# Attention in 128-token blocks ahead of an MLP: loads, transposes and scores by block, with rings of tiles

## The chip, the cores and the metric

One core of one Trainium2 chip. The metric is the device time of one execution in microseconds (us), the median of several fast runs. The span of a profile is shorter than the measured time of the same execution: 378.2 against 379.9 us before.

## The reference

Sliding-window attention with a linear distance bias (8 batches, 8 heads, 576 tokens, head size 64, window 128), whose output goes into an MLP with a squared ReLU (4608 tokens, 512 to 2048 to 512).

```python
scores = scale * np.matmul(q, k.transpose(0, 1, 3, 2))
mask = (rel >= 0) & (rel < 128)                      # rel = query - key position
scores = np.where(mask, scores + bias[None], -1e9)   # bias = -slope[h] * |rel|
attn = softmax(scores)
x = np.matmul(attn, v)            # -> (4608, 512), heads side by side
h = np.maximum(x @ w_in, 0.0)
out = (h * h) @ w_out
```

## The kernel before

The program is a list of small tasks (one instruction each, with the engine, an estimated length in ns, dependencies and a priority key, lower first). A list scheduler in the kernel file puts them in an order once, at build time; every engine then runs its instructions in exactly that order, and waits in place when the data is not there. So the estimated lengths decide the order, and only the order. PE is the matrix engine; it writes its results to PSUM, which this program uses as eight banks. An "eviction" is the copy of a finished bank by VectorE or ScalarE.

K and Q of a batch come in as two halves of four heads, 72 partitions of 8 tokens each. VectorE reorders them, PE transposes them in 16-fold pieces of 72 columns, and VectorE and ScalarE copy each finished bank out.

```python
def load(key, ns, emit, deps=(), acq=()):
    return plan.add({"POOL": 1000.0}, key, emit, deps, acq, dma=ns)   # figures for the scheduler
# K/Q half: 1900 ns; V, 128 tokens: 2050 ns; a quarter of w_in 3100 ns, of w_out 3300 ns
...
base_t = s_b - 256 - 16 if b > 1 else s_b - 4000 + 1000 * b      # key of a batch's transposes
base_s = s_b - 128 - 16 if b else -2000                          # key of its scores
...
for r in range(R):                         # R = 8 transposes of 72 columns fill one bank
    nc.tensor.transpose(slot.tile[:, r * RP:(r + 1) * RP],
                        sl.tile[:, r, 2 * cj:2 * cj + 2].rearrange("p h d -> p (h d)"), ident[0:RP, 0:RP])
...
add_evac(kT[p2][c][:, 0:S], [last, t_pad[p2]], 0, 128, t_k[c], {"DVE": dve(576)})   # after the last of the eight
...
nc.tensor.matmul(slot.tile[:, 0:2 * nq].rearrange("p (c q) -> p c q", c=2),         # scores, by key block
                 kT[p2][c][:, kb * 128:(kb + 1) * 128], qp[p2][c][:, :, kb * 128:kb * 128 + nq], ...)
```

The MLP works on groups of 512 tokens: matmuls `h` (w_in), ReLU on ScalarE, square on VectorE, matmuls `o` (w_out). Group 0 needs the tokens of blocks 0 to 3 of batch 0. The attention of later batches is woven between the matmuls of earlier MLP groups. The eight banks are shared out as two each for `h`, `o`, scores (`s`) and everything else of attention (`att`).

The softmax here doesn't subtract the row's maximum and nothing guards it: scores larger than these inputs give would overflow.

## Time and profile before

| | before |
|---|---|
| measured, first three runs | 379.1 us (377.2 to 379.2) |
| span of the profile | 378.2 us |
| first MLP matmul starts | 53.0 us |
| PE streaming work in all (see below) | 318.7 us |
| of it before the first MLP matmul | 12.5 us |
| PE time lost after the first MLP matmul | 15.1 us |
| of that, ahead of input transposes | 3.8 us |

"PE streaming work" and "time lost" are worked out from the start times of the matmuls in the trace. From 60 to 280 us the usual distance from one start to the next is 216 ns for 512 columns, 56 for 128 and 29 for 65, which is N/2.4 + 2.5 ns within a nanosecond or so. The 72-column transposes of the kernel before are the exception: mostly 35 ns apart where the formula has 32.5, so that some 1.3 us of its streaming counts as lost here. The sum by the formula over all matmuls is the streaming work; what the distance to the next start has more than that is lost. This tells more than the busy share, because in the trace, which models the ends of matmuls, one counts as busy for some 0.17 us beyond its streaming (0.38 us for 512 columns, 0.22 for 128).

These lines are from the page of the kernel before: busy time by engine; PE in 40 slices of the span (a 9 is 90% or more); the engines' shares of the chain that ended last.

```profile
PE 343.4 (91%) x2560; PEld 178.6 (47%) x2560; DVE 231.6 (61%) x620; ACT 199.7 (53%) x381; POOL 75.1 (20%) x103
...
PE   0567589989999999999999999999999999999995
...
PE 79%; DVE 10%; ACT 6%; DMA 2%; issue 2%; POOL 0%; ACTq 0%; POOLq 0%
```

PE is busy in nearly the whole span except the first six slices, which are 57 us. The same by stretches (length, then the busy us of PE, weight loads, VectorE, ScalarE and GpSimd with counts, the clock, DMA):

```profile
core 0: us, PE busy (x) PEld busy (x) DVE busy (x) ACT busy (x) POOL busy (x), PEclk, DMA share, GB/s
0.00:53.00 53.00, 27.62 (x242) 16.59 (x243) 37.80 (x93) 23.09 (x45) 36.75 (x56) 0.82 1.52 167
...
60.00:300.00 240.00, 235.01 (x1876) 123.83 (x1874) 168.51 (x454) 143.30 (x275) 36.83 (x45) 1.00 0.45 63
```

From 60 to 300 us PE is busy for 235.0 of 240 us. The first 53 us hold 242 of 2560 matmuls. What they wait for is in the timeline of VectorE (start, length, instruction). `xT` is the output of attention for one block of tokens; the reordering copies `r_` belong to batch 1's transposition:

```profile
35.62 0.41 DVE L466 COPY xT<-xp 128x512 bf16<-128x512 bf16 x1
35.95 0.68 DVE L327 COPY r_445<-q_70 72x2048 bf16<-72x2048 bf16 x1
36.55 0.87 DVE L327 COPY r_462<-k_71 72x2048 bf16<-72x2048 bf16 x1
...
52.47 0.42 DVE L466 COPY xT<-xp 128x512 bf16<-128x512 bf16 x1 [0.33 <-PE xp L459]
```

The copy at 35.6 us is the third of the four blocks that group 0 needs. The fourth is copied out only at 52.5 us: between them the engines reorder, transpose and copy out batch 1. The first MLP matmul follows at once (timeline of PE):

```profile
52.98 0.61 PE L493 MATMUL h<-xT,w_in_sb 128*128 128x512 bf16 x1
```

These are the first rows of the list of PE's waits from 60 to 300 us (who waited for whom: us in total, times, longest). It shows small, scattered waits:

```profile
engine line waited for: us in total, times, longest us
PE pv L424 <- DVE qp_3_77 L357: 0.9, 1, 0.9
PE pv L424 <- DVE xT L466: 0.5, 1, 0.5
...
```

### The profile page before, as it was taken

How to read it: one execution, taken by the hardware profiler on the slowest of the kernel's cores; microseconds unless marked ns; L12 is line 12 of the kernel's file. 1: busy time of each engine (PE TensorE's matmuls, PEld its weight loads, DVE VectorE, ACT ScalarE, POOL GpSimd, SP SyncE). 2: the span in 40 equal slices, each digit the busy share in tenths (PEclk: the TensorE clock that was granted, in tenths of full speed). 3: DMA queues.
4: the chain of work that ended last, by engine and by line, in shares of the span. 5: the costliest groups of instructions: out<-in, count | busy, mean ns of one | idle time of the engine just before them, and what ended most of it. 6: DMA issues, size and time to landing. Idle time of an engine off the chain costs nothing.

```text
span 378.2 us, 6568 instructions
## 1 busy us (share of the span) xinstructions
PE 343.4 (91%) x2560; PEld 178.6 (47%) x2560; DVE 231.6 (61%) x620; ACT 199.7 (53%) x381; POOL 75.1 (20%) x103
## 2 busy tenths in 40 slices
PE   0567589989999999999999999999999999999995
PEld 0324345545455545555555554555555554444442
DVE  5878568767687777657775677476767754222200
ACT  1373447545574757347654656475657743434411
POOL 8995422203112112120211020101000000000000
PEclk9998569999999999999999999999999999999999
DMA  7999995839364717562919260531310001100112
GB/s 100 147 204 161 205 172 24 111 45 162 79 62 64 97 11 105 88 88 42 112 22 126 43 79 4 83 44 30 20 57 10 21 29 45 38 29 28 55 57 83
DMA packets 59742, 28.22 MB, mean 75 GB/s; under 512 B 41792, under 2 KB 55104, under 8 KB 59712
## 3 DMA queue, kind: packets, MB, share of 16 engines
q0 software_dynamic: 54528, 18.37, 49.2%
q1 hardware_dynamic: 5184, 9.44, 6.8%
q8 instruction: 20, 0.33, 0.4%
q14 instruction: 10, 0.08, 0.1%
HBM read 36.70 MB, written 9.44 MB: 122 GB/s over the span
## 4 chain that ended last, share of the span: by engine, by line
PE 79%; DVE 10%; ACT 6%; DMA 2%; issue 2%; POOL 0%; ACTq 0%; POOLq 0%
PE o L522 31%; PE h L493 29%; PE ps_s L384 7%; PE pv L424 5%; PE tp L343 4%; DMA k_71<-in_k_dram 2%; PE xp L459 2%; ACT P_91 L395 1%; DVE qp_1_75 L357 1%; DVE qp_2_76 L357 1%; DVE qp_0_74 L357 1%; ACT qp_2_76 L359 1%; ACT rt L501 1%; DVE qp_1_79 L357 1%; DVE qp_0_78 L357 1%
## 5 line engine op out<-in xcount | busy, mean ns | idle before, releaser
L493 PE MATMUL h<-xT,w_in_sb 128*128 128x512 bf16 x576 | 188.4, 380 | 0.1
L522 PE MATMUL o<-w_out_sb,g 128*128 128x512 bf16 x576 | 183.6, 379 | 0.5 <-ACT osb L533 0.3
L501 ACT ACTIVATE rt<-h 128x512 bf16<-128x512 f32 x144 | 85.5, 599 | 75.1 <-PE h L493 64.1
L507 DVE TENSOR_TENSOR g<-rt 128x512 bf16<-128x512 bf16 x144 | 59.3, 416 | 49.9 <-ACT rt L501 48.1
L522 PEld LDWEIGHTS <-g 128*128 128x128 bf16 x576 | 54.3, 98 | 40.4 <-issue 2.5
L493 PEld LDWEIGHTS <-w_in_sb 128*128 128x128 bf16 x576 | 53.0, 98 | 31.6 <-issue 2.1
L533 ACT ACTIVATE osb<-o 128x512 f32<-128x512 f32 x36 | 21.4, 597 | 33.3 <-PE o L522 27.8
L440 DVE RECIPROCAL rec<-pv 128x4 f32<-128x4 f32 (+1 forms) x80 | 13.2, 175 | 32.4 <-PE pv L424 18.9
L290 POOL DMA_DIRECT2D vt_73<-in_v_dram x20 | 17.4, 876 | 52.8 <-PE pv L424 31.5
L279 POOL DMA_DIRECT2D q_70<-in_q_dram x16 | 12.7, 795 | 72.1 <-DVE r_2514 L327 9.9
L395 ACT ACTIVATE P_91<-ps_s 128x512 bf16<-128x512 f32 (+2 forms) x40 | 20.0, 515 | 10.5 <-PE ps_s L384 10.2
L290 POOL DMA_DIRECT2D vt_72<-in_v_dram x20 | 17.6, 883 | 35.6 <-PE pv L424 27.2
L395 ACT ACTIVATE P_93<-ps_s 128x512 bf16<-128x512 f32 (+2 forms) x40 | 19.5, 516 | 9.2 <-PE ps_s L384 8.9
L395 ACT ACTIVATE P_92<-ps_s 128x512 bf16<-128x512 f32 (+2 forms) x40 | 19.5, 515 | 7.1 <-PE ps_s L384 6.3
L395 ACT ACTIVATE P_90<-ps_s 128x512 bf16<-128x512 f32 (+2 forms) x40 | 19.4, 516 | 5.5 <-PE ps_s L384 5.0
L466 DVE COPY xT<-xp 128x512 bf16<-128x512 bf16 (+1 forms) x40 | 15.7, 394 | 8.5 <-PE xp L459 6.2
L424 PEld LDWEIGHTS <-P_93 128*128 128x128 bf16 x144 | 13.7, 101 | 12.7 <-issue 3.5
L424 PEld LDWEIGHTS <-P_90 128*128 128x128 bf16 x144 | 13.9, 102 | 11.4 <-issue 2.9
L424 PEld LDWEIGHTS <-P_91 128*128 128x128 bf16 x144 | 13.6, 100 | 11.4 <-issue 2.2
L424 PEld LDWEIGHTS <-P_92 128*128 128x128 bf16 x144 | 13.4, 99 | 10.2 <-issue 1.0
L459 PE MATMUL xp<-ident,x_94 128*128 128x128 bf16 x80 | 17.2, 227 | 0.7 <-DVE x_94 L445 0.6
L407 DVE TENSOR_TENSOR P_91<-P_91,masks 128x512 bf16<-128x512 bf16 (+2 forms) x40 | 14.0, 363 | 5.7 <-ACT P_91 L395 5.3
(200 smaller groups left out, 555.3 us busy)
## 6 DMA issues: line engine op xcount, KB each, us to landing
out_dram<-osb SPq DMA_DIRECT2D x36, 256.0 KB, 2.0
k_71<-in_k_dram POOLq DMA_DIRECT2D x16, 288.0 KB, 6.7
q_70<-in_q_dram POOLq DMA_DIRECT2D x16, 288.0 KB, 5.5
vt_72<-in_v_dram POOLq DMA_DIRECT2D x16, 128.0 KB, 6.0
w_in_sb<-in_moe_w_in_dram POOLq DMA_DIRECT2D x4, 512.0 KB, 8.2
vt_73<-in_v_dram POOLq DMA_DIRECT2D x16, 128.0 KB, 5.3
w_out_sb<-in_moe_w_out_dram POOLq DMA_DIRECT2D x4, 512.0 KB, 11.0
vt_72<-in_v_dram POOLq DMA_DIRECT2D x4, 64.0 KB, 4.7
```

Source lines behind the costliest of these rows:

```text
L290: nc.gpsimd.dma_start(vt[i][0:n, kb, :, 0:D], v[b, :, kb * 128:kb * 128 + n, :].rearrange("h s d -> s h d"))
L357: nc.vector.tensor_copy(o, s_)
L384: nc.tensor.matmul(slot.tile[:, 0:2 * nq].rearrange("p (c q) -> p c q", c=2), kT[p2][c][:, kb * 128:(kb + 1) * 128], qp[p2][c][:, :, kb * ...
L395: nc.scalar.activation(Pt[sP.idx][:, 2 * c:2 * c + 2, 0:nq], slot.tile[:, 0:2 * nq].rearrange("p (c q) -> p c q", c=2), AF.Exp, bias=0.0, ...
L424: nc.tensor.matmul(slot.tile[:, hi * (D + 1):(hi + 1) * (D + 1)], Pt[sp.idx][:, h, off:off + 128], vt[i][:, kk, h, :], start=st, stop=en)
L459: nc.tensor.transpose(slot.tile[:, c * 128:(c + 1) * 128], xt[sx.idx][:, c * 128:(c + 1) * 128], ident)
L466: nc.vector.tensor_copy(xT[:, :, t0:t0 + n], slot.tile[:, 0:512].rearrange("p (c t) -> p c t", c=C)[:, :, 0:n])
L493: nc.tensor.matmul(slot.tile, w_in_sb[:, cc, fc * 128:(fc + 1) * 128], xT[:, cc, g * 512:(g + 1) * 512], start=cc == 0, stop=cc == C - 1)
L501: nc.scalar.activation(srt.tile, slot.tile, AF.Relu, bias=0.0, scale=1.0)
L507: nc.vector.tensor_tensor(sg.tile[:, fc, :], srt.tile, srt.tile, op=ALU.mult)
L522: nc.tensor.matmul(slot.tile, sg.tile[:, fc, t * 128:(t + 1) * 128], w_out_sb[:, fc, :], start=fc == 0, stop=fc == FCB - 1)
L533: nc.scalar.activation(so.tile, slot.tile, AF.Copy)
```

## The change

The intent: stream attention in blocks of 128 tokens, so that the first output tokens, and with them the MLP, start early. K, Q and V of a block come in natural order (128 tokens on 128 partitions). Eight transposes of 128 columns, K's four and Q's four, fill one bank. Scores go by query block, so that a block needs only its own K and the K before it. All tiles are small rings. The core of the diff, with cuts marked by `...` and comments added:

```diff
-    q8 = const.tile([RP, H, R * D], BF16)
-    k8 = const.tile([RP, H, R * D], BF16)
...
+    size = {"kn": 4, "qn": 4, "v": 6, "kT": 4, "qp": 3, "P": 3, "x": 2}
+    kn = ring("kn", size["kn"], [128, d_model])
...
-        return plan.add({"POOL": 1000.0}, key, emit, deps, acq, dma=ns)
+        return plan.add({"POOL": 900.0}, key, emit, deps, acq, dma=ns)
-            t_win[n] = load(key + n, 3100.0, emit)
+            t_win[n] = load(key + n, 2550.0, emit)
...
+                nc.gpsimd.dma_start(o, src[b, :, kb * 128:kb * 128 + n, :].rearrange("h s d -> s h d"))
+            t_in[m, nm] = load(key + 0.01 * i, 1050.0 * n / 128, emit, ...)
...
+        due = (b * S + kb * 128 + n) / 4 - 192 - 150
...
+        for i in range(2 * C):                       # K's four, then Q's four, one bank
+                nc.tensor.transpose(slot.tile[:, i * 128:(i + 1) * 128], src[:, (i % C) * 128:(i % C + 1) * 128], ident)
+            if i == C - 1:
+                last_k = last
+        t_k = plan.add(both if first else {"DVE": both["DVE"]}, due - 56, evac_k, [last_k], [], [slot])
...
-                        kT[p2][c][:, kb * 128:(kb + 1) * 128],
-                        qp[p2][c][:, :, kb * 128:kb * 128 + nq],
+            for part, mk in parts:                   # the key block before, and this one
+                        kT[sk_of[mk].idx][:, c, :], qp[sq.idx][:, c, :, 0:n], start=True, stop=True)
...
+        slot_x = Slot("o" if first else "att")       # batch 0 borrows the MLP's banks
```

It also gives the scheduler new figures for loads: 1050 ns for 128 tokens where V had 2050, 2550 for a weight quarter where it had 3100 and 3300, 900 for an issue where it had 1000. The diff changes other figures too (a matmul N/2.4 + 1.5 ns where it had + 3, the constants 800 and 1300 where they had 2500 and 3000), lets either VectorE or ScalarE make batch 0's evictions, and drops some clearing of tiles on GpSimd.

## The prediction

> **What bounds the kernel now.** The page shows PE busy 91% of 378 us; from 60 to 300 us the stretch table has it busy 235.0 of 240 us at full clock. In the timeline warm matmuls start about 216 ns (512 columns), 56 ns (128), 32 ns (72) and 30 ns (65) apart, as the Trainium skill states ("TensorE: Matmul & The Clock Gate", Back-to-back issue gap: N/2.4 + 2.5 ns). Summed with that spacing (estimate): MLP 1152 x 216 = 248 us, scores 27.7, weighted values 17.0, input transposes 16.6, output transposes 8.9: about 318 us. So some 60 us of the span is not streaming.
>
> Where it lies: the first MLP matmul starts at 53.0 us. Before it PE has done only about 12.7 us of warm work (128 transposes, 28 scores, 69 values, 16 output transposes): 40 us lost. After it about 16 us are lost in gaps and cold clock, and 3.7 us are the tail. There the chain of waits runs over K loads, the 72x2048 reorder copies (0.68 us each, one 3.08 us) and the 576-column strided evictions (0.75 us DVE, 0.65 us ACT): batch 0 needs all heads of all 576 tokens before its first score, and the whole transposition of batch 1 (34 to 50 us) goes in front of the first MLP matmul.
>
> **The change.** Removes 32 reorder copies (24 us of DVE), 512 transposes of 72 columns, 64 DVE and 32 ACT evictions (48 and 21 us). Adds 320 transposes of 128 columns (17.8 us of PE against 16.6) and 120 evictions of up to 512 columns (0.42 us DVE, 0.6 us ACT, like the xT and exp instructions now). Scores become 288 matmuls of half the width for 160: same columns. DVE falls by some 35 us; PE's sum becomes about 320 us: nothing won there. K and Q now move as 128-byte packets like V: 110,592 instead of 36,864. In the trace they take 40 ns, but with several loads queued one engine starts one each 15 to 16 ns: about 1 us a load, like the 0.88-0.96 us in which POOL issues one. 120 loads need some 110 us of 300: no new bottleneck, but a block costs 2.9 us of issue at the start.
>
> **The critical part: the start.** Block 0 needs only its K and Q (landed near 7 us), transposes, evictions and masks: first exp near 8.5 us (21.4 now), first output tokens near 14. Then a block needs 4 exps of 0.6 us and an eviction on ACT (3 us), and about 4 us of shared DVE work, against 2.9 us of loads: 3.5 to 4 us a block. Four blocks feed group 0: first MLP matmul near 28 us, w_in's first quarter landed before that. PE has then done 9 us. Left are 311 us of streaming, the tail of 3.7 and about 14 us lost: cold clock, ACT and DVE shared by batch 1's attention and the first MLP groups and smaller gaps. 28 + 311 + 18 = 357 us: 22 us (6%) faster. Range 349 to 366. Chances: faster 0.94, same 0.05, slower 0.01.
>
> **What would show it.** First MLP matmul at 25 to 32 us; no 72-partition copies; DVE busy near 195 us; PE busy over 95% from 60 to 300 us; streaming sum within 2 us of before; SWDGE packets about 115,000 or more; POOL about 120 us.
>
> **What would make it wrong.** 128-byte loads slower at the start (30 ns apart instead of 15), which pushes w_in past 28 us; POOL issuing slower while DVE works; PE in program order stalling on a late block or on DVE and ACT between 28 and 60 us; w_out, issued behind batch 1's 15 loads, landing after 45 us.

## The result, and the profile after

365.8 us (four runs, 365.7 to 366.0), against 378.4 us before: the ratio is 0.967, with a 95% interval of 0.964 to 0.970. A ratio here is the mean time of one kernel's fast runs over the mean of the other's in the same rounds, so it is not quite the ratio of the medians quoted. The change is 12.6 us faster; 22 us had been forecast, and the time lies 0.2 us inside the upper end of the range.

| | predicted | before | after |
|---|---|---|---|
| time | 357 (349 to 366) | 378.4 us | 365.8 us |
| first MLP matmul | 25 to 32 us | 53.0 us | 29.5 us |
| streaming work in all | within 2 us of before | 318.7 us | 320.6 us |
| of it before the first MLP matmul | 9 us | 12.5 us | 8.7 us |
| lost after the first MLP matmul | about 14 us | 15.1 us | 19.0 us |
| of that, ahead of input transposes | not told | 3.8 us | 13.8 us in 39 places |
| VectorE busy | near 195 us | 231.6 us | 193.8 us |
| GpSimd busy | about 120 us | 75.1 us | 108.4 us |

The "39" counts places where more than 0.15 us were lost. Of these, 35 stand ahead of one of Q's transposes, in 34 of the 35 blocks whose transposes follow the first MLP matmul; what is lost ahead of Q's transposes is 12.1 us. The other four are K's of block 5 (1.6 us, of which 1.0 for the load of its K). The page of the changed kernel:

```profile
PE 338.9 (93%) x2496; PEld 187.5 (51%) x2496; DVE 193.8 (53%) x593; ACT 205.1 (56%) x394; POOL 108.4 (30%) x137
...
PE   2677899999999999999999999999999999999995
...
PE 76%; issue 7%; POOL 5%; DMA 4%; DVE 4%; ACT 2%; POOLq 0%; ACTq 0%
```

PE shows 7 to 8 tenths from the third slice on and reaches a 9 with the sixth, that is from 45.5 us, where the kernel before does so from 57. The DMA queue that GpSimd feeds carries 116,736 packets where it had 54,528, at the same bytes. By stretches, with the columns of before:

```profile
0.00:29.50 29.50, 16.00 (x160) 11.54 (x160) 17.40 (x61) 18.31 (x39) 23.60 (x35) 0.97 1.48 138
...
60.00:300.00 240.00, 234.76 (x1826) 132.82 (x1825) 143.46 (x439) 146.56 (x282) 65.86 (x80) 1.00 0.70 68
```

The first stretch is 23.5 us shorter. But from 60 to 300 us PE is busy for 234.8 us, hardly other than the 235.0 of before, although VectorE has 25 us less to do there. The start, in the timelines of VectorE, ScalarE and PE:

```profile
16.25 0.41 DVE L280 COPY xT<-xp 128x512 bf16<-128x512 bf16 x1
...
24.23 0.60 ACT L282 ACTIVATE xT<-xp 128x512 bf16<-128x512 bf16 x1
26.94 0.60 ACT L282 ACTIVATE xT<-xp 128x512 bf16<-128x512 bf16 x1
28.83 0.60 ACT L282 ACTIVATE xT<-xp 128x512 bf16<-128x512 bf16 x1 [1.29 <-PE pv L378]
...
29.48 0.58 PE L450 MATMUL h<-xT,w_in_sb 128*128 128x512 bf16 x1 [0.47 <-ACT xT L282]
```

The fourth block's output comes at 28.8 us instead of 52.5. And this is the whole list of PE's waits from 60 to 300 us, with the same columns as before:

```profile
PE tp L301 <- DVE kT_86 L280: 1.1, 4, 0.3
PE tp L301 <- DVE kT_85 L280: 1.0, 4, 0.3
PE tp L301 <- DVE kT_84 L280: 0.7, 3, 0.3
PE tp L301 <- DVE kT_87 L280: 0.5, 2, 0.3
```

Scattered waits have given way to a single kind: an input transpose waits for VectorE's copy of `kT`. One such place, in the timeline without the weight loads (cuts marked by `...`; `tp<-ident,kn_72` is the last of K's four transposes, `qn_76` is Q):

```profile
64.06 0.22 PE L301 MATMUL tp<-ident,kn_72 128*128 128x128 bf16 x1
...
64.32 0.42 DVE L280 COPY kT_86<-tp 128x512 bf16<-128x512 bf16 x1 [0.87 <-PE tp L301]
64.33 0.19 PE L378 MATMUL pv<-vt_79,P_93 128*128 128x65 bf16 x1
...
64.79 0.22 PE L301 MATMUL tp<-ident,qn_76 128*128 128x128 bf16 x1 [0.27 <-DVE kT_86 L280]
64.85 0.38 PE L479 MATMUL o<-w_out_sb,g 128*128 128x512 bf16 x1
```

PE starts a 65-column matmul at 64.33 us and would be free for the next 29 ns later. The next is Q's first transpose, at 64.79. In between VectorE copies K out of the same bank, 64.32 to 64.74. The two touch different columns of it. The Trainium skill ("PSUM — Partial Sum Buffer", PSUM bank collisions raise a hardware error) says that two engines may not be in one bank and the same quarter of the partitions at the same time, whichever columns they touch, and that a program must guard by bank and quarter and not by address. This program does, with a semaphore that Q's transpose waits on (the first of Q's in 22 of the 35 places, the second in 11, the third in 2). That the guard is needed is the page's statement; every kernel run here keeps it, so no run shows the collision.

### The profile page after: what moved, and what is told of

The parts are those of the page before. It is cut to its first block, busy times and chain, and to the rows that moved or that the text cites. A ratio compares the mean times of both kernels' runs of the same rounds, so it can differ in the third digit from the quotient of the medians.

```text
span 364.2 us, 6535 instructions
## 1 busy us (share of the span) xinstructions
PE 338.9 (93%) x2496; PEld 187.5 (51%) x2496; DVE 193.8 (53%) x593; ACT 205.1 (56%) x394; POOL 108.4 (30%) x137
## 3 DMA queue, kind: packets, MB, share of 16 engines
q0 software_dynamic: 116736, 18.36, 68.3%
## 4 chain that ended last, share of the span: by engine, by line
PE 76%; issue 7%; POOL 5%; DMA 4%; DVE 4%; ACT 2%; POOLq 0%; ACTq 0%
PE h L450 30%; PE o L479 30%; PE ps_s L337 6%; PE tp L301 5%; PE pv L378 4%; DMA kn_71<-in_k_dram 3%; PE xp L417 2%; DMA qn_74<-in_q_dram 1%; DVE kT_86 L280 1%; DVE kT_87 L280 1%; DVE kT_84 L280 1%; DVE kT_85 L280 1%; POOL w_in_sb L238 1%; POOL kn_70 L262 1%; POOL vt_79 L262 0%
## 5 line engine op out<-in xcount | busy, mean ns | idle before, releaser
L450 PE MATMUL h<-xT,w_in_sb 128*128 128x512 bf16 x576 | 199.4, 382 | 0.7 <-ACT xT L282 0.5
L479 PE MATMUL o<-w_out_sb,g 128*128 128x512 bf16 x576 | 190.8, 379 | 0.2
L450 PEld LDWEIGHTS <-w_in_sb 128*128 128x128 bf16 x576 | 54.8, 98 | 34.8 <-issue 7.0
L399 DVE RECIPROCAL rec<-pv 128x4 f32<-128x4 f32 (+1 forms) x80 | 14.4, 179 | 35.7 <-PE pv L378 34.1
L355 ACT ACTIVATE P_91<-ps_s 128x512 bf16<-128x512 f32 (+1 forms) x56 | 27.1, 505 | 8.8 <-PE ps_s L337 8.5
L355 ACT ACTIVATE P_92<-ps_s 128x512 bf16<-128x512 f32 (+1 forms) x52 | 26.3, 518 | 8.2 <-PE ps_s L337 7.4
L355 ACT ACTIVATE P_93<-ps_s 128x512 bf16<-128x512 f32 (+1 forms) x52 | 25.9, 515 | 7.2 <-PE ps_s L337 6.5
L363 DVE TENSOR_TENSOR P_91<-P_91,masks 128x512 bf16<-128x512 bf16 (+1 forms) x56 | 19.7, 361 | 6.5 <-ACT P_91 L355 6.2
L363 DVE TENSOR_TENSOR P_93<-P_93,masks 128x512 bf16<-128x512 bf16 (+1 forms) x52 | 18.7, 365 | 4.8 <-ACT P_93 L355 4.4
L363 DVE TENSOR_TENSOR P_92<-P_92,masks 128x512 bf16<-128x512 bf16 (+1 forms) x52 | 18.4, 365 | 4.9 <-ACT P_92 L355 4.4
L280 DVE COPY xT<-xp 128x512 bf16<-128x512 bf16 (+1 forms) x37 | 14.6, 395 | 8.2 <-PE xp L417 5.8
L417 PE MATMUL xp<-ident,x_94 128*128 128x128 bf16 x80 | 17.5, 224 | 0.0
L417 PE MATMUL xp<-ident,x_95 128*128 128x128 bf16 x80 | 17.1, 223 | 0.0
L404 DVE TENSOR_TENSOR x_94<-pv,rec 128x256 bf16<-128x256 f32 (+1 forms) x40 | 16.7, 416 | 0.5
L262 POOL DMA_DIRECT2D kn_73<-in_k_dram x10 | 8.4, 844 | 28.3 <-PE tp L301 20.9
```

Source lines behind the costliest of these rows:

```text
L280: nc.vector.tensor_copy(o, i)
L355: nc.scalar.activation(view(Pt[sP.idx][:, 2 * c:2 * c + 2]), view(slot_s.tile.rearrange("p (c t q) -> p c t q", c=2, t=2)), AF.Exp, bias=0 ...
L363: nc.vector.tensor_tensor(pt, pt, view(masks[:, 2 * c:2 * c + 2]), op=ALU.mult)
L417: nc.tensor.transpose(slot_x.tile[:, c * 128:(c + 1) * 128], xt[sx.idx][:, c * 128:(c + 1) * 128], ident)
L450: nc.tensor.matmul(slot.tile, w_in_sb[:, cc, fc * 128:(fc + 1) * 128], xT[:, cc, g * 512:(g + 1) * 512], start=cc == 0, stop=cc == C - 1)
L479: nc.tensor.matmul(slot.tile, sg.tile[:, fc, t * 128:(t + 1) * 128], w_out_sb[:, fc, :], start=fc == 0, stop=fc == FCB - 1)
```

## The experiments

Three theories of the 9 us that were missing against the forecast are named A to C in the expectations, and two pairs on where the gain comes from D to G. Every run passed the comparison with the reference. One of them (long rows) passed although its K and Q are read in the wrong order; so this comparison does not catch a wrong order in the scores, and a pass proves less than it seems to. Of that run the time counts, not the result. Times of the kernel before, in the rounds that they shared, were 377.0 us for the first four runs told below and 378.7 to 378.8 for the others, on another chip; so compare ratios, and not times, across the two sets.

| run | time, us | ratio to before (95%) | first MLP matmul | lost after it |
|---|---|---|---|---|
| changed kernel | 365.8 | 0.967 (0.964 to 0.970) | 29.5 | 19.0 |
| K's copy after Q's transposes | 361.6 | 0.957 (0.954 to 0.961) | 31.5 | 12.0 |
| the same from batch 1 on | 356.9 | 0.942 (0.938 to 0.945) | 29.6 | about 10 |
| two banks | 356.9 | 0.946 (0.944 to 0.947) | 27.5 | 10.7 |
| two banks, w_in shared out | 355.8 | 0.940 (0.937 to 0.943) | 32.4 | about 7 |
| long rows (wrong result) | 363.4 | 0.964 (0.961 to 0.966) | 28.1 | 17.1 |
| before, batch 1 later | 385.0 | 1.021 (1.018 to 1.023) | 38.9 | 31.5 |
| before, new figures | 380.7 | 1.006 (1.003 to 1.009) | 51 to 52 | about 16 |
| changed, old figures | 383.1 | 1.013 (1.009 to 1.017) | 35.3 | about 29 |

"About" stands where 46 of PE's records are missing from the trace. They make up some 10 us of streaming work (all kernels of one structure have the same sum), which is taken off the apparent loss.

### K's copy after Q's transposes

```diff
-        t_k = plan.add(..., evac_k, [last_k], [], [slot])
+        t_k = plan.add(..., evac_k, [last], [], [slot])
```

> Changed kernel, one word different: the K eviction is ordered after all eight transposes of its bank instead of after the four of K. Theory A (the 9 us missing against the prediction are spent because Q's last three transposes write a bank from which VectorE still copies K, so PE waits in nearly every block): the 39 waits of input transposes on VectorE are gone; the time lost ahead of input transposes after the first MLP matmul falls from 13.8 us to under 4; time 353 to 358 us, ratio to the kernel before 0.933 to 0.946 (the changed kernel: 0.967). Rival B (VectorE is simply late, being shared): K comes still later, scores wait instead of transposes, time 363 to 369 us.

Measured: 361.6 us. The time lost ahead of input transposes went from 13.8 to 2.0 us, as theory A says, and everything lost after the first MLP matmul from 19.0 to 12.0. But the first MLP matmul came 2.0 us later, and the time fell between the two expectations. So A's mechanism is shown, and this cure has a price of its own at the start; the run that does it from batch 1 on, below, looks for it.

### Two banks

```diff
-        slot = Slot("h" if first else "att")
+        slots = [Slot("h" if first else "att") for _ in range(2)]      # one for K, one for Q
...
-                    slot.tile = psum.tile([128, 1024], BF16, tag=slot.tag, name="tp")
+                if i % C == 0:
+                    sl.tile = psum.tile([128, 1024], BF16, tag=sl.tag, name="tp")
```

> Changed kernel with K and Q transposed into two separate banks, K's eviction still ordered after K's transposes. Theory A: the waits on VectorE ahead of Q's transposes go too, but a block now takes five turns of the two shared banks instead of four, so some waits for a free bank appear: time 354 to 361 us. Rival B: as slow as the changed kernel or slower, 364 to 369 us.

Measured: 356.9 us, inside what A expects. Here K's copy still follows K's transposes directly, and VectorE has the same work, so "VectorE is late" (B) falls. All of PE's waits from 60 to 300 us that the list shows:

```profile
PE o L481 <- DVE g L466: 0.3, 1, 0.3
```

No input transpose is left in it, and no wait for a free `att` bank either, which had been feared. The same stretch by engines, with the columns of before:

```profile
60.00:300.00 240.00, 239.53 (x1875) 136.12 (x1874) 149.60 (x446) 148.52 (x288) 66.87 (x81) 1.00 0.71 69
```

PE is busy for 239.5 us where it was for 234.8. The time lost in this stretch, worked out from the starts, went from 11.3 to 3.7 us (the kernel before: 11.9). The largest loss left is near the start (timeline of PE): right behind the first MLP matmul stands a transpose of block 5, whose K is loaded behind the whole of w_in.

```profile
30.82 0.29 PE L302 MATMUL tp<-ident,kn 128*128 128x128 bf16 x1 [2.92 <-DMA kn<-in_k_dram]
```

### Long rows (wrong on purpose)

```diff
+                    rows = src[b].rearrange("h (s e) d -> (h s) (e d)", e=8)
+                    nc.gpsimd.dma_start(dst[sl.idx][0:n], rows[kb * 128:kb * 128 + n, :])     # K and Q
```

> Changed kernel, wrong result on purpose: K and Q are read as rows of 512 contiguous numbers, so their packets are 1024 bytes instead of 128, at the same bytes and the same number of loads; V unchanged. Rival C (the missing time is the cost of three times as many small packets): 5 us or more faster than the changed kernel, 355 to 360 us. Theory A: only the start gains, since blocks 1 to 3 land somewhat earlier: 363 to 366 us, first MLP matmul at 28 to 29.5 us, the 13.8 us of waits ahead of input transposes stay within 2 us.

Measured: 363.4 us, 2.4 us less than the changed kernel; by the ratios 0.3 to 0.4% of 378 us, so 1 to 2 us. The waits ahead of transposes stayed at 12.7 us. So C is not where the 9 us went. The queue has 52,224 packets instead of 116,736. Two issues on GpSimd (V and K) in the timeline:

```profile
4.27 0.92 POOL L263 DMA_DIRECT2D vt<-in_v_dram  x1
5.18 0.55 POOL L266 DMA_DIRECT2D kn<-in_k_dram  x1
```

K's and Q's issues take 0.52 to 0.61 us where they take 0.88 to 0.94 in the changed kernel, V's stay near 0.92, and the first MLP matmul comes 1.4 us earlier. Which of issuing and packets sets the pace of the loads in the changed kernel, its trace does not tell: GpSimd issues one load each 0.87 us at the start, and from 30 to 40 us, when several issued loads are waiting behind w_in, they land one each 0.86 us (13.1 to 13.4 ns from packet to packet on each of 16 engines, against 13.6 for 1024 packets in 0.87 us). The Trainium skill ("DMA: Bandwidth & Descriptors", Specifications) puts the smallest transfer for full rate at 512 bytes; here 128-byte packets cost this kernel 1 to 2 us in all; from 60 to 300 us PE is busy for 234.8 of 240 us with them.

### The kernel before, batch 1 later

```diff
-        base_t = s_b - 256 - 16 if b > 1 else s_b - 4000 + 1000 * b
+        base_t = s_b - 256 - 16 if b else s_b - 4000
```

> Kernel before, one key different: batch 1's transposes get the priority rule of all later batches instead of one above batch 0's scores. Theory D (most of the earlier start comes from order: in the kernel before, the last output tokens of group 0 stand behind batch 1's transposes): first MLP matmul at 38 to 43 us instead of 53, time 366 to 372 us, ratio 0.965 to 0.982. Rival E (it comes from streaming in blocks, and this key alone gives nothing, because the work put off is missed later): time 375 to 380 us.

Measured: 385.0 us, slower than either expected. The early start came as D says, 38.9 us. It was lost again, and more: 31.5 us after it against 15.1. These are the `h` matmuls by stretches in this run (PE and weight loads only), and then in the kernel before:

```profile
core 0: us, PE busy (x) PEld busy (x), PEclk, DMA share, GB/s
53.00:70.00 17.00, 9.05 (x27) 2.35 (x27) 1.00 1.31 67
70.00:90.00 20.00, 0.00 (x0) 0.00 (x0) 0.81 0.62 95
```

```profile
53.00:70.00 17.00, 12.55 (x39) 3.60 (x40) 0.95 1.26 73
70.00:90.00 20.00, 7.92 (x26) 2.09 (x25) 1.00 0.59 94
```

From 70 to 90 us there is not one: MLP group 1 has no tokens, since batch 1 is transposed, scored and normalised only then. PE is busy for 14.6 of these 20 us, and its clock falls to a mean of 0.66 from 70 to 80 us and of 0.50 from 90 to 100 us. So theory D falls as a way to gain, in the one order that was tried. My reading: with whole batches, an early start of the MLP is borrowed from the next batch; with blocks what has been put off is one block.

### The kernel before with the new load figures

```diff
-        return plan.add({"POOL": 1000.0}, ...)          +  900.0
-            t_win[n] = load(key + n, 3100.0, emit)      +  2550.0   (w_out: 3300 -> 2550)
-                ... load(key, 1900.0, ...)              +  1450.0
-            t_vt[b, kb] = load(key, 2050.0 * ...)       +  1050.0 * ...
```

> Kernel before, with only the change's new load figures given to its scheduler (a 128-token load 1050 ns instead of 2050, a weight quarter 2550 instead of 3100, an issue 900 instead of 1000). Theory F (a good part of the gain is the better figures): first MLP matmul well before 53 us and 368 to 373 us. Rival G (the gain is the block streaming; the old order still transposes all of batch 1 before the first MLP matmul): first MLP matmul at 48 to 54 us, 373 to 380 us.

Measured: 380.7 us, 0.6% slower; that is just above what G expects. The first MLP matmul hardly moved (its weights load at 51.0 us). On the old structure the figures gain nothing.

### The changed kernel with the old load figures

```diff
-            t_in[m, nm] = load(key + 0.01 * i, 1050.0 * n / 128, ...)
+            t_in[m, nm] = load(key + 0.01 * i, 2050.0 * n / 128, ...)      # and 3100, 1000
```

> Changed kernel with the old load figures given to its scheduler (2050, 3100 and 1000 ns). Theory F (the figures matter): the scheduler puts all of MLP group 0 ahead of most of batch 1 and of the first output matmul: 369 to 376 us. Rival G (streaming alone): within 3 us of the changed kernel, 363 to 369 us.

Measured: 383.1 us, worse than either expected, and 1.3% slower than the kernel before. The old kernel had no load of 128 tokens of K or Q (its halves had 1900 ns), so V's figure stands for all three, and w_out has 3100 instead of its old 3300. Nothing in this program but the order differs from the changed kernel; GpSimd's first 15 loads are issued at the same times within 0.1 us. Busy times from 60 to 100 and from 100 to 200 us (PE, weight loads, VectorE, ScalarE, GpSimd, as above), the changed kernel first, then this run:

```profile
60.00:100.00 40.00, 39.24 (x313) 22.34 (x312) 26.07 (x80) 25.66 (x52) 14.03 (x18) 1.00 0.87 77
100.00:200.00 100.00, 97.28 (x760) 55.28 (x759) 59.89 (x181) 60.89 (x117) 34.51 (x41) 1.00 0.83 75
```

```profile
60.00:100.00 40.00, 36.20 (x262) 19.99 (x264) 20.87 (x64) 20.14 (x40) 11.27 (x14) 0.96 0.71 62
100.00:200.00 100.00, 93.44 (x727) 53.82 (x740) 58.23 (x176) 58.88 (x114) 33.92 (x41) 1.00 0.85 79
```

PE runs short of work up to 200 us (the counts of this run read low by its share of the 46 missing records). What this run shows is that the figures alone did it; how is my reading of the order: with 120 loads of 2050 ns each the scheduler takes the loads for the limit, and puts the attention of later batches where the data would come if that were so. It does not come so late, and PE stands in the meantime on orders that no longer fit: the first `o` matmul is at 61.1 us, against 46.0.

### K's copy after Q's transposes, from batch 1 on

```diff
-        t_k = plan.add(..., evac_k, [last_k], [], [slot])
+        t_k = plan.add(..., evac_k, [last_k if first else last], [], [slot])
```

> Changed kernel, K's eviction after all eight transposes only from batch 1 on; in batch 0 as in the changed kernel. The run that did it everywhere came to 361.6 us with its first MLP matmul 2 us later than the changed kernel. If that delay was K's eviction held back at the start: first MLP matmul at 29 to 30 us, 357.5 to 360.5 us. If the delay has another cause: 360.5 to 363 us.

Measured: 356.9 us, first MLP matmul at 29.6 us: the 2 us at the start are back, and the time is a little better than expected (0.942 against 0.957 for the same cure everywhere). In the list of PE's waits from 60 to 300 us there are three left, of 0.2 us each.

### w_in shared out

Built on two banks: the loads of blocks 5 and 6 are issued between the quarters of w_in.

```diff
-            t_win[n] = load(key + n, 2550.0, emit)
+            t_win[n] = load(key + 10 * n, 2550.0, emit)
-        load_block(m, -7e5 + m)
+        load_block(m, -8e5 + 5 + 10 * (m - NKB) if m < NKB + 2 else -7e5 + m)
```

> Two-bank version, with the loads of blocks 5 and 6 issued between the four quarters of w_in instead of behind them. In the two-bank run PE stands 3.1 us behind its first MLP matmul for block 5's K. If that wait is a real loss: it goes to under 0.7 us, time 352 to 355.5 us (two-bank run: 356.9). If the time is only moved (the later quarters of w_in land late, or ACT and DVE bound this stretch): 356 to 359 us, with a wait for w_in or for exps in its place.

Measured: 355.8 us, between its two expectations, and a ratio of 0.940 against 0.946: a small gain, and not a clean one. The 3.1 us wait is gone, but the scheduler, told of the earlier loads, put block 5's and 6's transposes ahead of the first MLP matmul, which came at 32.4 instead of 27.5 us. Less was lost afterwards (about 7 us instead of 10.7). Most of the wait was moved.

### Block 5 alone, on two banks and on the later copy

The same with block 5 only (`NKB + 1`), on two banks and on "K's copy after Q's transposes, from batch 1 on".

> Two-bank version with only block 5's three loads issued right behind the first quarter of w_in (the run that also put block 6 there traded the 3.1 us wait for a first MLP matmul 5 us later). If the wait for block 5's K can be taken away without that: first MLP matmul at 27.5 to 29.5 us, time 352.5 to 355.5 us, ratio 0.932 to 0.941. If the stretch is bound by ACT and DVE, as the last run suggests: first MLP matmul at 30 us or later and 355 to 358 us.

> Version with K's eviction after all eight transposes from batch 1 on (356.9 us, ratio 0.942), with block 5's loads right behind the first quarter of w_in too. It had only 0.9 us of wait for block 5's K, so at most 1 to 1.5 us is to be had: 354.5 to 357.5 us, ratio 0.937 to 0.945; first MLP matmul 29 to 31 us.

Measured: 358.5 us (0.948, 0.945 to 0.951) and 358.8 us (0.948, 0.946 to 0.951). The first lies 0.5 us above the second of its expectations, with the first MLP matmul at 31.3 us as told there. The second is a miss: a cure for a wait of 0.9 us made the kernel slower than without it (0.942), with the first MLP matmul at 32.3 us. In both the scheduler again moved block 5 ahead of it.

## Why the prediction was right or wrong

The sign was right, the time is in the range by 0.2 us, and the earlier start came from where it was forecast; the gain was forecast at 22 us and is 12.6.

- **"First MLP matmul near 28 us"; "PE has then done 9 us".** Measured: 29.5 and 8.7 us. Right, 1.5 us off. The way there was less even than told: the first output copy came at 16.3 us (near 14 forecast), and the next three 8.0, 2.7 and 1.9 us later where 3.5 to 4 us a block had been forecast. That the sum of the three agrees is in part luck.
- **"311 us of streaming, the tail of 3.7".** Measured: 311.9 (320.6 less 8.7) and 3.9 us. Right. Half as wide scores and wider transposes cost PE 1.9 us by the formula, less with the 35 ns of the old transposes.
- **"About 14 us lost".** This is the step that failed in size. 19.0 us were lost, 13.8 of them ahead of input transposes, 12.1 ahead of Q's. The prediction costed the new evictions by their length and the transposes by theirs, and counted on VectorE's 35 us of relief. It did not ask who else uses the bank: before, each bank was full before anyone copied from it; now K's copy is released after half of the eight transposes, and nearly each time holds up the other half. What the prediction did name (cold clock, shared engines, small gaps) came to some 7 us instead of 14: two errors in part cancelled, and that the total was only 5.0 us off is luck. Moving the copy behind all transposes, or splitting the bank in two, takes 10 to 12 us of it away (2.0 and 4.0 us left, 3.1 of the latter for a load), and two of the three versions that take only that wait away run at 356.9 us. That this is the time forecast for the change itself is again in part luck: they lose about 10 us after the first MLP matmul, not 14.
- **357 us as a time.** The sum (28 + 311 + 14 + 3.7 = 356.7) was one of the span, and a measured time is 1.6 to 2 us above it. Together: 1.5 (start) + 0.9 (streaming) + 5.0 (lost) + 0.2 (tail) + 1.8 (span to time) = 9.4 us; the profiled run, at 366.0 us, is 9.3 above the sum.
- **"Batch 0 needs all heads of all 576 tokens before its first score".** Wrong for the score: before, the first one ran at 15.7 us, with 23 of batch 0's 64 transposes still to come. Its exp did wait, until 21.4 us: on ScalarE it stands behind the last evictions of batch 0. The other half of the sentence, batch 1's transposition in front of the first MLP matmul, was the part that counted: three of four output blocks were there at 36.0 us, and the fourth was copied from 52.5 on.
- **"No new bottleneck" in the loads.** Right in the main: long rows gain 1 to 2 us. One load was late, that of block 5's K (1.0 us lost in the changed kernel, 3.1 with two banks). Packets (116,736), GpSimd (108 us against about 120) and VectorE (193.8 us) came as told.
- **Not foreseen:** that the gain hangs on the scheduler's load figures, which the prediction read in the diff and did not cost. The structure with the old figures is 1.3% slower than the kernel before, the old structure with the new figures 0.6% slower, the two together 3.3% faster. And an early start got by order alone, with whole batches, was given back with interest in the one run that tried it.

What stays open: whether the program could do without the guard at all (no run tries it); whether the best version, two banks with w_in shared out (355.8 us, faster than both kernels of the change), is really better than the others within 1% of it, because each small edit makes the scheduler shift the first MLP matmul by several us; what the other changes in the diff are worth alone; and which of VectorE and ScalarE would bound the stretch from 28 to 45 us if the order were ideal.

## What to carry to other kernels

Where two operands share one PSUM bank and the program guards the bank, as here, its first reader holds up its next writer: either let the copy wait for the last writer, or give each operand its own bank, and look for it as many small waits of one kind rather than one large one. In a statically ordered kernel the assumed durations are part of the code: after a change of what is loaded, check them against the trace, since a good structure in the order of wrong figures was slower here than the old one. An earlier start did not pay here where a whole batch was put off in its favour; ask what is put off, and whether its data can still arrive in time.

## What the Trainium skill lacked or had wrong

- "TensorE: Matmul & The Clock Gate", Back-to-back issue gap: it gives about 81 ns (128 columns) and 131 ns (512) for a sustained stream of weight load and matmul pairs, and calls N/2.4 + 2.5 ns the figure of a single one. In these traces every matmul has its own weight load (2560 of each before, 2496 after), and the usual distance in the stream is 55 to 56 ns for 128 columns and 215 to 216 ns for 512, so the formula holds for the stream (less well for 72 columns: mostly 35 against 32.5). The page disagrees with itself here: its section "Wait — 56ns, not 53.3ns?" measures 55.6 and 215.7 ns for back-to-back matmuls, as these traces do.
- "PSUM — Partial Sum Buffer", PSUM bank collisions raise a hardware error: the page states the rule, the error and the remedy (another bank), and not what the guard costs when a bank is copied out half full: here 0.19 to 0.43 us of PE's time in 34 of 35 blocks, 12.1 us of 364 in all, which two banks or a later copy remove.
- "DMA: Bandwidth & Descriptors", Anatomy of one DMA: it calls the time of descriptor generation small and variable, and gives no figure for it. Here GpSimd needs 0.87 to 0.95 us to issue a load of 1024 packets of 128 bytes, and 0.52 to 0.61 us for one of 128 rows of 1024 bytes.
- "Perfetto Trace Analysis", Identifying the Most-Contended Engine: it calls the busy share of matmuls a bad measure of the distance from roofline, and gives no size for what the share hides. Here PE is busy for 234.8 of 240 us from 60 to 300 us, where 11.3 us are lost by the starts, and the list of waits shows 0.27 us for the one that cost 0.43.
